# Weight conversion of the first quarter from attention tile 12 instead of 18, in a one-core attention and two-MoE kernel

## The chip, the cores and the metric

The kernel runs on one core of a Trainium2 chip. The metric is the device time of one execution in microseconds, given as the median of several runs. A profiled execution has its own time and, beside it, the span from its first to its last instruction.

## The reference

Clustered attention feeds a dense MoE block, which feeds a routed MoE block with eight experts.

```python
attn: B=2, H=8, S=768, D=64
  mask   = q_assign[:, :, :, None] == k_assign[:, :, None, :]   # argmax over 16 centroids
  scores = where(mask, q @ k.T / sqrt(D), -1e9)
  attn   = softmax(scores) @ v                                  # -> x of 1536 x 512
moe:   x = (relu(x @ w_in) ** 2) @ w_out                        # w_in 512 x 2048, float64
moe2:  do_compute = x @ w_skip > 0;  e = argmax(x @ w_gate)
       y = prob[e] * (relu(x @ w1[e]) @ w2[e]);  out = x + y
```

## The kernel before, in words

**Attention.** The 16 heads (two batches of eight) are handled two at a time, as 8 pairs of 12 tiles, 96 tiles of 128 queries by 768 keys. A loop over i (line 683) writes the order of every engine's work by hand: `ORDER` (line 24) lists the operations of one turn. In turn i, PE makes the scores of tile i + 3 (`S`, line 513), DVE takes their row maximum nm (`M`, line 520), ACT the exponential p (`E`, line 529). Of tile i itself PE transposes both halves into PSUM tiles pt (line 555; three PSUM tiles in rotation), ACT rounds them to ph (line 569), DVE takes the rest pl (line 578), and PE multiplies both with the values (line 588). Every 12 turns the operands of the next pair are prepared in between: PE transposes q and k (line 342), ACT copies them out (line 430), POOL splits them (lines 134 and 350), DVE finds the clusters (lines 380, 382, 399), POOL splits v (lines 134 and 413). Every third turn an output block is copied by ACT (lines 604, 605) and for the second head scaled by POOL (lines 607, 608). In attention PE, ACT, DVE and POOL keep the hand-written order; the order of SP's queue of transfers is set by a planner.

**Conversion of weights.** `weights` (line 183) is a generator that turns float64 weights of the first MoE block into a high and a low part, in four quarters of four units. A unit is 17 steps: for a w_in block and then for a w_out block, one step each for the transfer into a staging tile st (line 157, three staging tiles), one ACT operation (line 164), four DVE operations (lines 166, 169, 171, 174), the high part and the low part on POOL (lines 134 and 180); the 17th step closes the unit. The first quarter's 68 steps are spread over 96 turns: 17 steps in 24 turns (line 666, operation `D`, which comes after the values' first matmuls and before the second half's transposes).

```python
            if op == "D" and i >= CONV0:
                convert((i + 1) * CONV1 // 96 - i * CONV1 // 96)
```

The loop runs to i = 98. From line 693 on the last turns also split the attention's output for the first MoE block (line 230), and from i = 92 they do its first two steps (line 248 into sc).

**First MoE block.** A loop over 64 steps s (line 1107) makes, with PE, a hidden block (`gemm1`, lines 248 to 251), then two steps later its product with w_out (`gemm2`, line 1091). Step s of the first chunk needs unit s + 1 of the weights. After each step five more conversion steps are written (line 1116), until all four quarters are done. Here PE alone keeps its written order, and a planner orders ACT, DVE, POOL and SP, which may put an operation of this block between those of the attention's last turns. A staging transfer from step 3 on is held back by a one-element ACT copy (line 155).

**The rest.** Routing, and then eight experts, whose weights are loaded once the routing has named the first expert.

Of the kernel before, what the change touches and what calls it, by code (L numbers as in the profile page):

```python
# [28 lines left out]
SCALES = 1  # L29
SLAG = 2  # L30
ALB = 2
CONV0 = 18
CONV1 = 68
WARM = (9,1,1,2,2,2,4)
LOOK = 3
# [17 lines left out]
def clustered_attention_moe(  # L53
# [147 lines left out]
    def convert(n):  # L201
        for _ in range(n):
            if next(wgen, None) == "unit":
                wdone[0] += 1
# [57 lines left out]
    with ExitStack() as actx:  # L262
# [270 lines left out]
        def scales(n, c):  # L533

            su = su_t.pop((n, c)).rearrange("p t (h o) -> p t h o", o=1)
            nc.vector.tensor_scalar_add(su, su, 1e-9)
            nc.vector.reciprocal(out=su, in_=su)
            rr = sc_g[n, c] = alp.tile([128, G], F32, name="rr", bufs=2)
            nc.vector.tensor_copy(out=rr.rearrange("p (t h d) -> p t h d", t=GT, h=2),
                                  in_=su.to_broadcast([128, GT, 2, 64]))  # L540
# [93 lines left out]
        def micro(op, i):  # L634
# [26 lines left out]
            if op == "Z":  # L661
                m = i + LA - SLAG
                if 0 <= m < NQ and tiles[m][1] == 1 and m % GT == GT - 1:
                    scales(tiles[m][0], m // GT % 2)
            if op == "D" and i >= CONV0:
                convert((i + 1) * CONV1 // 96 - i * CONV1 // 96)
# [599 lines left out]
```

## Time and profile before

| what | us |
|---|---|
| median of 3 runs | 686.53 |
| lowest and highest run | 683.21, 688.05 |
| the profiled execution | 684.3 |
| its span | 682.5 |

The share of the granted TensorE clock is 0.989 over the span. Attention fills the span up to about 266 us, the first MoE block to about 530 us, the experts the rest. Busy time is that of an engine's own instructions; idle time before an instruction is put down to what released it. PE, DVE, ACT and POOL are the matmul, vector, scalar and GpSimd engines, and SP's queue issues most transfers.

### The profile page before, as it was taken

Reading aid. Unit: us, or ns where it says so; the run is one execution under the profiler, and the core shown is the slowest. Engines: PE = TensorE matmul, PEld = TensorE weight load, DVE = VectorE, ACT = ScalarE, POOL = GpSimd, SP = SyncE. Lnnn points to the kernel's source line nnn. Section 1 sums busy time; section 2 is a strip of 40 time slices with the busy share of each in tenths; the row PEclk is TensorE's granted clock in tenths of the full one; section 3 lists DMA queues with packets and bytes.
Section 4 is the critical chain, followed back from the end, with each engine's and each line's share of the span. In section 5 each row is a group of like instructions: output and inputs, shape, how many; then the busy total and the mean of one; then the engine's idle time right before and its main releaser. Section 6 shows DMA issues by size and latency. Waiting matters only on the chain. (4 is left out here: it accounts for less than half of the span.)

```text
span 682.5 us, 11258 instructions
## 1 busy us (share of the span) xinstructions
PE 648.4 (95%) x3769; PEld 566.0 (83%) x3769; DVE 477.4 (70%) x928; ACT 415.7 (61%) x846; POOL 253.7 (37%) x329
## 2 busy tenths in 40 slices
PE   7899899999999998999999999999999797999994
PEld 6788888989898887999998999999888575888883
DVE  4787899999999999654456455522244688899950
ACT  5799889989998984544433333322323375778830
POOL 4816264544736346643343443511010103113110
PEclk9899999999999999999999999999999989999998
DMA  5867764665746100123122312101222697999900
GB/s 130 190 150 154 185 142 122 150 157 127 164 123 139 41 1 9 63 66 104 63 78 62 108 63 62 40 0 47 93 93 94 216 315 252 345 356 362 367 13 23
DMA packets 72034, 89.90 MB, mean 132 GB/s; under 512 B 32384, under 2 KB 43584, under 8 KB 71968
## 3 DMA queue, kind: packets, MB, share of 16 engines
q1 hardware_dynamic: 68096, 84.12, 42.5%
q0 software_dynamic: 1440, 3.01, 1.3%
q10 hardware_dynamic: 2432, 1.97, 0.9%
q8 instruction: 32, 0.52, 0.3%
q14 instruction: 34, 0.28, 0.1%
HBM read 62.18 MB, written 9.44 MB: 105 GB/s over the span
## 5 line engine op out<-in xcount | busy, mean ns | idle before, releaser
L578 DVE TENSOR_TENSOR pl<-pt,ph 128x384 fp32r<-128x384 f32 x192 | 103.5, 551 | 19.2 <-ACT ph L569 18.0
L255 ACT ACTIVATE r<-hps 128x384 f32<-128x384 f32 x62 | 30.5, 492 | 120.7 <-PE hps L248 115.7
L555 PE MATMUL pt<-ident,p 128*128 128x128 f32 x576 | 95.9, 276 | 3.9 <-DVE pl L578 2.8
L513 PE MATMUL sc<-B,A 80*128 80x384 f32 (+1 forms) x384 | 91.8, 361 | 2.0 <-ACT p L529 1.8
L569 ACT CAST ph<-pt 128x384 fp32r<-128x384 f32 x192 | 89.7, 481 | 6.6 <-PE pt L555 5.9
L520 DVE TENSOR_REDUCE nm<-sc 128x1 f32<-128x768 f32 x96 | 91.0, 948 | 2.5 <-PE sc L513 2.5
L258 DVE TENSOR_TENSOR hl<-r,hh 128x384 fp32r<-128x384 f32 x62 | 36.7, 591 | 76.4 <-POOL hh L134 76.0
L529 ACT ACTIVATE p<-sc,nm 128x768 f32<-128x768 f32 x96 | 87.3, 910 | 4.4 <-DVE nm L520 4.3
L555 PEld LDWEIGHTS pt<-ident,p 128*128 128x128 f32 x576 | 70.4, 141 | 18.3 <-DVE pl L578 10.9
L134 POOL TENSOR_SCALAR hh<-r 128x384 fp32r<-128x384 f32 x62 | 35.4, 571 | 134.3 <-ACT r L256 114.9
L1091 PE MATMUL acc<-woh,hh 128*128 128x512 f32 x186 | 74.3, 400 | 0.0
L1091 PE MATMUL acc<-wol,hh 128*128 128x512 f32 x186 | 73.5, 395 | 0.0
L588 PE MATMUL av<-ph,vs 128*128 128x384 f32 x192 | 73.0, 380 | 0.1
L1091 PE MATMUL acc<-woh,hl 128*128 128x512 f32 x186 | 72.9, 392 | 0.0
L513 PEld LDWEIGHTS sc<-B,A 80*128 80x128 f32 (+1 forms) x384 | 63.2, 191 | 6.3 <-ACT p L529 6.2
L588 PE MATMUL av<-pl,vs 128*128 128x384 f32 x192 | 65.2, 339 | 0.6 <-DVE pl L578 0.6
L248 PE MATMUL hps<-A,wil 128*128 128x384 f32 x184 | 61.9, 336 | 2.0 <-POOL wil L180 2.0
L248 PE MATMUL hps<-A,wih 128*128 128x384 f32 x184 | 62.4, 339 | 0.0
L248 PE MATMUL hps<-B,wih 128*128 128x384 f32 x184 | 61.9, 337 | 0.0
L164 ACT ACTIVATE u<-st 128x512 f32<-128x512 f32 x32 | 21.7, 677 | 32.9 <-DMA st<-in_moe_w_in_dram 25.6
L1091 PEld LDWEIGHTS acc<-woh,hl 128*128 128x128 f32 x186 | 35.2, 189 | 7.8
L1091 PEld LDWEIGHTS acc<-woh,hh 128*128 128x128 f32 x186 | 35.2, 189 | 5.7 <-DVE xc L1099 0.2
(260 smaller groups left out, 1484.1 us busy)
## 6 DMA issues: line engine op xcount, KB each, us to landing
xc<-in_moe_w_dram SPq DMA_DIRECT2D x34, 512.0 KB, 5.5
st<-in_moe_w_dram SPq DMA_DIRECT2D x30, 512.0 KB, 5.8
st<-in_moe_w_in_dram SPq DMA_DIRECT2D x64, 128.0 KB, 2.9
st<-in_moe_w_out_dram SPq DMA_DIRECT2D x16, 512.0 KB, 3.9
A<-hi SPq DMA_DIRECT2D x30, 192.0 KB, 3.5
B<-hi SPq DMA_DIRECT2D x30, 192.0 KB, 4.0
qn<-in_q_dram SPq DMA_DIRECT2D x16, 192.0 KB, 3.5
vn<-in_v_dram SPq DMA_DIRECT2D x16, 192.0 KB, 2.6
```

The costliest lines, as they stand in the source:

```text
L134: nc.gpsimd.tensor_scalar(out=o, in0=i, scalar1=1.0, scalar2=0.0, op0=ALU.mult, op1=ALU.add)
L248: nc.tensor.matmul(out=hps, lhsT=wi[w][:, c, f * 128:(f + 1) * 128], rhs=xhl[ch][a][:, c], start=(n == 0), stop=(n == 3 * KD - 1))
L255: nc.scalar.activation(out=r, in_=hps, func=AF.Relu)
L258: nc.vector.tensor_tensor(out=hl, in0=r, in1=hh.bitcast(F32), op=ALU.subtract)
L513: nc.tensor.matmul(out=sc[:, c, 0:384], lhsT=A[h][0:kk, a, t * 128:(t + 1) * 128], rhs=Bk[h][0:kk, a, c * 384:(c + 1) * 384], start=(a == ...
L520: nc.vector.tensor_reduce(out=nm_t[i], in_=sc_t[i][:, :, 0:384], op=ALU.max, axis=AX.XY, negate=True)
L529: nc.scalar.activation(out=p, in_=sc[:, :, 0:384], func=AF.Exp, bias=nm, scale=1.0, accum_out=su_t[n, c][:, t, h:h + 1])
L555: nc.tensor.transpose(out=pt[:, c], in_=p_t[i][:, n, c * 128:(c + 1) * 128], identity=ident)
L569: nc.scalar.copy(out=block(i, n)[by_pool].bitcast(F32) if by_pool else block(i, n)[0], in_=pt_t[i, n])
L578: nc.vector.tensor_tensor(out=pl, in0=pt_t.pop((i, n)), in1=ph.bitcast(F32), op=ALU.subtract)
L588: nc.tensor.matmul(out=av, lhsT=vs[:, c, 2 * h:2 * h + 2].rearrange("p x d -> p (x d)"), rhs=r[:, c], start=(c == 0 and i == 0), stop=(c = ...
L1091: nc.tensor.matmul(out=acc, lhsT=h2[a][:, i * 128:(i + 1) * 128], rhs=wo[w][:, f], start=(f == 0 and n == 0), stop=(f == NF - 1 and n == 2))
```

## The change

The constant that says in which turn of the attention's loop the conversion begins goes from 18 to 12. The pace, 17 steps in 24 turns, stays.

```diff
-CONV0 = 18
+CONV0 = 12
 CONV1 = 68
```

## Rows read from the trace of the kernel before

**Rows 1.** The page, part 1: busy us (share of the span) xinstructions.

```profile
PE 648.4 (95%) x3769; PEld 566.0 (83%) x3769; DVE 477.4 (70%) x928; ACT 415.7 (61%) x846; POOL 253.7 (37%) x329
```

**Rows 2.** Waits, 241.9 to 275 us: us in total, times, longest.

```profile
PE hps L248 <- POOL wil L180: 2.0, 1, 2.0
```

**Rows 3.** Timeline, PE, 270.6 to 273.5 us: start, length, instruction, idle before.

```profile
270.69 0.33 PE L248 MATMUL hps<-A,wih 128*128 128x384 f32 x1
273.03 0.44 PE L248 MATMUL hps<-A,wil 128*128 128x384 f32 x1 [2.01 <-POOL wil L180]
```

**Rows 4.** Timeline, DVE then POOL, 256 to 273 us.

```profile
259.69 0.42 DVE L169 TENSOR_SCALAR l<-st 128x512 int32<-128x512 int32 x1
...
263.13 1.41 DVE L171 SCALAR_TENSOR_TENSOR l<-st,l 128x512 int32<-128x512 int32 x1
...
267.79 0.99 DVE L174 SCALAR_TENSOR_TENSOR u<-u,l 128x512 int32<-128x512 int32 x1
...
269.12 0.79 POOL L134 TENSOR_SCALAR wih<-u 128x512 fp32r<-128x512 f32 x1
...
271.26 1.71 POOL L180 TENSOR_TENSOR wil<-u,wih 128x512 fp32r<-128x512 f32 x1
```

**Rows 5.** Windows, stretches of six turns, then the tail and the MoE block.

```profile
core 0: us, PE busy (x) PEld busy (x) DVE busy (x) ACT busy (x) POOL busy (x), PEclk, DMA share, GB/s
...
61.50:77.00 15.50, 13.98 (x94) 12.95 (x93) 12.33 (x23) 13.40 (x32) 5.96 (x10) 1.00 0.69 156
77.00:93.70 16.70, 15.86 (x111) 13.60 (x109) 15.79 (x28) 14.71 (x35) 8.37 (x10) 1.00 0.71 175
93.70:107.60 13.90, 13.90 (x96) 12.89 (x95) 13.04 (x24) 13.42 (x32) 7.23 (x11) 1.00 0.53 123
107.60:123.30 15.70, 15.55 (x110) 13.41 (x109) 15.07 (x28) 14.49 (x35) 8.82 (x10) 1.00 0.60 141
123.30:137.00 13.70, 13.70 (x94) 12.70 (x93) 12.25 (x23) 13.23 (x32) 7.20 (x11) 1.00 0.62 145
...
241.90:255.00 13.10, 12.57 (x77) 11.17 (x78) 12.98 (x25) 11.40 (x27) 5.40 (x7) 1.00 0.01 2
255.00:266.40 11.40, 10.83 (x67) 9.47 (x65) 10.62 (x23) 8.14 (x18) 3.77 (x5) 1.00 0.01 1
...
275.00:330.00 55.00, 55.00 (x279) 50.03 (x278) 29.29 (x51) 24.00 (x53) 26.53 (x32) 1.00 0.25 77
```

**Rows 6.** Timeline, DVE: the four conversion operations of unit 2's w_in block.

```profile
138.37 0.42 DVE L166 TENSOR_SCALAR u<-u 128x512 f32<-128x512 f32 x1
...
140.49 0.94 DVE L169 TENSOR_SCALAR l<-st 128x512 int32<-128x512 int32 x1
...
143.92 1.37 DVE L171 SCALAR_TENSOR_TENSOR l<-st,l 128x512 int32<-128x512 int32 x1
...
149.36 0.68 DVE L174 SCALAR_TENSOR_TENSOR u<-u,l 128x512 int32<-128x512 int32 x1
```

**Rows 7.** Timeline, POOL: one split of v, one output scaling.

```profile
126.17 0.74 POOL L413 TENSOR_TENSOR vs<-vn,vs 128x256 fp32r<-128x256 f32 x1
...
143.74 1.00 POOL L607 TENSOR_TENSOR xc<-xc,al 128x384 f32<-128x384 f32 x1 [2.59 <-ACT xc L605]
```

**Rows 8.** Timeline, PE: where it stood idle between 137 and 153.7 us.

```profile
142.73 0.55 PE L555 MATMUL pt<-ident,p 128*128 128x128 f32 x3 [0.21 <-DVE pl L578]
...
145.81 0.55 PE L555 MATMUL pt<-ident,p 128*128 128x128 f32 x3 [0.47 <-DVE pl L578]
```

**Rows 9.** Timeline, SP's queue and PE, 41.6 to 47 us.

```profile
41.66 1.31 SPq L293 DMA_DIRECT2D qn<-in_q_dram  x2
...
45.96 1.85 SPq L157 DMA_DIRECT2D st<-in_moe_w_in_dram  x4
46.23 0.52 PE L342 MATMUL tp<-ident,qn 128*128 128x128 f32 x3 [0.48 <-DVE pl L578]
```

**Rows 10.** Timeline, ACT: the first conversion operation.

```profile
70.87 0.68 ACT L164 ACTIVATE u<-st 128x512 f32<-128x512 f32 x1
```

## The prediction, made before the changed kernel ran

> **What bounds the kernel now.** I read the page first, then the waits around the end of attention, then windows of six turns, then the timeline of single engines. On the page PE is busy for 95% of the span [rows 1], so time can only be won where PE stands still, and lost where another engine makes it stand still. In the first MoE block PE never stops: 55.00 busy us in 55.00 [rows 5]. Whatever the change moves there is hidden, as long as the weights are there in time.
>
> At one place they are not. At 270.69 PE begins the block's step 3, which needs unit 4 of the weights, and then waits 2.01 us for its low part [rows 2, 3]. That low part is conversion step 59. The attention's loop writes 58 steps; the last ones come late: the DVE operations at 259.69, 263.13 and 267.79, the high part at 269.12, the low part at 271.26 for 1.71 us [rows 4]. The wait is set by where these steps are written, not by a transfer.
>
> In attention the windows fall into two kinds. From turn 21 on, six turns with the operands' preparation at their heart (turns 9 to 2 of 12, "heavy") take 16.70 or 15.70 us, and the six others ("light") take 13.90 or 13.70. In the light ones PE is busy all the time, DVE for 12.25 to 13.04 us and ACT for 13.23 to 13.42: three engines near their limit. In the heavy stretch of 16.70 PE stands still for 16.70 - 15.86 = 0.84 us [rows 5], and in the same stretch one pair later PE's idle places are two waits for pl, just behind two conversion operations that took 0.94 and 1.37 us [rows 6, 8]. The heavy stretch of 15.70 has hardly any idle.
>
> **The change part by part.** Step k is written in the first turn i in which the count of (i + 1) x 68 / 96 reaches k + 12 before, and k + 8 after. So every step moves up by four steps, between five and seven turns, and the loop writes 62 steps instead of 58.
>
> *What moves where.* Before, the w_in block's four DVE steps lay in turns 21, 22, 23 and 25, the w_out block's in 32, 33, 35 and 36, and so on every 24 turns: seven of eight in heavy stretches. After, they lie in 15, 16, 18 and 19, and in 26, 28, 29 and 31: seven of eight in light ones. ACT's operation goes the other way, from turns 19 and 31 to 14 and 25.
>
> *Heavy stretches that held a w_in block* (the row at 77.00, two more of the pattern at 137.00 and 197.10). They lose three or four DVE operations and keep or gain one of 0.42. PE's 0.84 idle us should go, and the stretch come to the 15.70 of its neighbour: 1.0 less. But ACT gains 0.68 us [rows 10] on 14.71, which makes 15.39 in 15.70, so I take 0.8. Three times: -2.4. Bounds: 0 (ACT takes over) and -3.0.
>
> *The other heavy stretches* lose DVE work that PE did not wait for and gain 0.68 us of ACT on 14.49: 15.17 in 15.70. A light stretch now runs with ACT at the same share without a PE stop. I take 0, with bounds -0.3 and +0.5 in all.
>
> *Light stretches that get a w_in block* (turns 39 to 44, row 123.30; two of them, and turns 15 to 20, row 61.50). The four DVE steps cost 0.42 + 0.42 + 0.69 + 0.68 = 2.2 us undisturbed, with 0.69 for line 171 as the half of its 1.37, near line 174's 0.68; or 0.42 + 0.94 + 1.37 + 0.68 = 3.4 as in rows 6. DVE's room is 13.70 - 12.25 = 1.45 us. So DVE lacks 0.75 to 1.95 us. Some is lent by the neighbours, since three transposed tiles are in flight, and the stretch loses 0.68 us of ACT work, for which DVE waits there. I take 0.6 each, bounds 0 and 2.0; the stretch at 61.50 has 15.50 - 12.33 = 3.2 of room and takes 0.3. Sum: +1.5.
>
> *Light stretches that get the rest of a w_out block* (row 93.70, three of them). They get 0.42 + 0.69 + 0.68, lose one operation of line 166, 0.42, and have 13.90 - 13.04 = 0.86 of room: lacking 0.5, or 1.7 if disturbed. I take 0.3, bounds 0 and 1.7. Sum: +0.9.
>
> In these light stretches POOL splits v, in pieces of 0.74 us, and scales outputs in pieces of 1.00 [rows 7]. In rows 6 and 7 the operation of 1.37 us ran beside such a scaling, at 143.92 and 143.74. The Trainium skill (SBUF — State Buffer, Who interferes with whom) has a DVE operation with two SBUF inputs, or one in a two-port mode, wait for the whole of a POOL instruction that began before it. By that rule lines 166 and 169, moved beside the split of v, would lose up to 0.74 us each, and the light w_in stretch would lack about 2.2 us. It speaks against the change, and the mechanism of the slower rival below is the same, worked out from rows.
>
> *The last full stretch* (turns 87 to 92, row 241.90). DVE is busy 12.98 of 13.10 us there, with the split of the attention's output beside its own work. It now gets the four DVE steps of unit 4's w_in block: 2.2 less 0.12 of room, +2.1. Nothing hides it, since DVE is the bound there. Bounds: +0.5 (the low part of the unit before it, on POOL, leaves the stretch, so DVE may run less disturbed) and +3.3.
>
> *The tail* (row 255.00). Those steps leave it. PE stood idle there for 11.40 - 10.83 = 0.57 us: -0.5, bounds 0 and -0.6.
>
> *The wait for unit 4.* Steps 58 and 59 are now written in turns 93 and 94, so the low part is ready before attention's matmuls end: -2.0. PE's next need, step 2's squares, is freed at the same time, as POOL no longer has the 0.79 and 1.71 us of rows 4 ahead of them. What follows is bound by PE, and the experts' loads start after the routing, so the gain is kept. Bounds: -2.0 and 0.
>
> *SP's queue.* Nothing keeps SP's written order, but the staging transfers stay between the same two loads of q, k and v: the first is written in turn 12, after the load of turn 7 and before that of turn 19. The queue's first four staging issues took 1.85 us right behind that load, and the load's q was just late, with PE idle for 0.48 us [rows 9]. I take 0, bounds 0 and +1.85.
>
> Sum: -2.4 + 0 + 1.5 + 0.9 + 2.1 - 0.5 - 2.0 = -0.4 us. Against the profiled execution's 684.3 that is 683.9. That execution lies 2.2 below the median of 686.53, so for a median I say 686.1.
>
> **The rivals.**
>
> *All hidden.* The lookahead lends DVE all it lacks: light stretches 0, last stretch +0.5. Then -2.4 + 0.5 - 0.5 - 2.0 = -4.4: 682.1. For it speaks that PE ran at 100% with DVE at 13.04 of 13.90; against it, that ACT and DVE are both near full there.
>
> *DVE becomes the bound of the light stretches.* Each moved operation meets POOL and is prolonged as in rows 6. Then w_in stretches lose 2.0 twice and 0.2 once, w_out stretches 1.7 three times, the last stretch 3.3, and the tail gives nothing: 4.2 + 5.1 + 3.3 - 2.4 - 2.0 = +8.2: 694.7, slower. It decides from the point where a light stretch grows past about 15 us. Against it: POOL is busy for only about 7.2 us of a light stretch, and some of that was its conversion work, which moves away.
>
> *The change doesn't do what it says.* The planner already lifts block-one work into attention's last turns; if it then puts other POOL work ahead of the low part, the wait stays: -0.4 + 2.0 = +1.6: 688.1.
>
> *SP's order.* The first staging transfer goes ahead of the load that is just late: -0.4 + 1.85 = +1.5: 688.0.
>
> **How the numbers follow.** Forecast 0.58, all hidden 0.20, DVE bound 0.12, the other two 0.05 each. Since 1%, about what a measurement of this kernel can tell from no change, is 6.9 us, only the DVE rival at its full price passes it, and the hidden one only if the measured median also falls low (the three runs lie 4.8 us apart). So faster 0.06, within 1% 0.84, slower 0.10. The range reaches down below the hidden case and up to where the DVE rival is half paid: 681.0 to 692.0.
>
> **What would show it.** Right: no wait of PE on line 180 near 270 us; heavy stretches all near 15.7 to 15.9; light ones 14.0 to 14.5, with PE's idle there put down to pl or ph; the stretch from the 91st row maximum some 2 us longer. Wrong: light stretches still at 13.7 to 13.9 (all hidden), or past 15 with DVE at 100% (DVE bound); heavy ones still at 16.7, which would mean that line 169 and line 171 were not the cause of PE's idle; a wait of PE on line 342 near 46 us longer than 0.48.

## The result, and the profile after

The changed kernel takes 693.83 us (median of 6 runs, 691.94 to 696.01) against 685.43 for the kernel before (6 runs): 1.0124 times, with an interval of 1.0099 to 1.0148. It is 8.4 us slower, and the forecast of 686.1 with a range up to 692.0 missed it. The profiled execution of the changed kernel took 696.01 us, with a span of 694.2.

On the page PE's busy time hardly moves; the span grows around it (as [rows 1]).

```profile
PE 652.2 (94%) x3769; PEld 568.5 (82%) x3769; DVE 479.1 (69%) x928; ACT 417.6 (60%) x845; POOL 253.4 (37%) x329
```

The windows of the changed kernel, cut at the starts of every sixth row maximum (the same turns as in [rows 5]; the columns are the same):

```profile
core 0: us, PE busy (x) PEld busy (x) DVE busy (x) ACT busy (x) POOL busy (x), PEclk, DMA share, GB/s
...
63.44:79.80 16.36, 14.25 (x92) 12.41 (x91) 14.83 (x27) 13.11 (x31) 6.70 (x11) 1.00 0.60 145
79.80:97.29 17.49, 16.18 (x115) 14.18 (x113) 14.96 (x26) 15.96 (x38) 9.38 (x11) 1.00 0.74 177
97.29:111.19 13.90, 13.01 (x88) 11.69 (x87) 13.69 (x26) 12.45 (x29) 6.88 (x11) 1.00 0.66 171
111.19:127.56 16.37, 16.21 (x116) 14.41 (x115) 13.73 (x24) 15.11 (x36) 7.97 (x10) 1.00 0.60 133
127.56:141.95 14.39, 13.51 (x90) 11.80 (x89) 14.11 (x27) 13.01 (x31) 6.91 (x11) 1.00 0.61 152
141.95:159.76 17.81, 16.41 (x118) 14.60 (x116) 15.04 (x26) 15.97 (x38) 9.36 (x11) 1.00 0.61 135
...
251.15:265.40 14.25, 12.65 (x76) 10.96 (x76) 14.25 (x27) 11.30 (x26) 5.65 (x8) 1.00 0.12 37
265.40:277.50 12.10, 11.22 (x59) 10.16 (x60) 8.86 (x20) 6.36 (x14) 3.76 (x5) 0.86 0.00 1
```

The reader is to see three things. The light stretches went about as forecast: those with the rest of a w_out block stayed at 13.90, with DVE at 13.69 (97.29), and those with a w_in block grew to 14.39, with DVE at 14.11 (127.56). The heavy ones that held a w_in block did the opposite of the forecast: instead of falling from 16.70 to 15.9 they grew to 17.49 and 17.81, though DVE does less in them (15.04 where it did 15.79). And the last full stretch has DVE busy for the whole 14.25.

From turn 21 on a stretch repeats to a few hundredths in the runs whose conversion steps lie in the same turns there: turns 21 to 26 took 16.69 in the kernel before and in two runs below (e8, e9), and 17.49 and 17.48 in the changed kernel and another (e7). Earlier ones do not: turns 9 to 14 took 17.20 in the kernel before, and 17.08 to 17.91 in four runs below that have the same steps as it up to turn 16 (e8 to e11). With that in mind the loss can be laid out by stretches, as the difference of the starts of two row maxima six tiles apart in the timeline (line 520):

| turns | 9-14 | 15-20 | 21-26 | 27-32 | 33-38 | 39-44 | 45-50 | 51-56 | 57-62 | 63-68 | 69-74 | 75-80 | 81-86 |
|---|---|---|---|---|---|---|---|---|---|---|---|---|---|
| before | 17.20 | 15.50 | 16.69 | 13.88 | 15.68 | 13.75 | 16.71 | 13.86 | 15.70 | 13.77 | 16.72 | 13.39 | 14.72 |
| after | 17.81 | 16.36 | 17.49 | 13.90 | 16.38 | 14.39 | 17.80 | 13.91 | 16.37 | 14.38 | 17.79 | 13.90 | 15.04 |

The differences add up to +7.95. From turn 87 to the last values' block (the 187th matmul of line 588 with ph) it is 23.94 against 21.05, +2.89. From the first matmul of the MoE block's step 2 to the first of its step 5 (line 248, hps from A and wih, the 1st and the 13th) it is 14.33 against 14.88, -0.55. What lies between and what follows is equal to 0.1. Before turn 9 the two profiled executions differ by 1.3 us; that part varies between kernels with the same start as well (first row maximum at 15.6 to 17.9).

PE stands still at two places in the stretch of turns 45 to 50. First PE's rows, then what DVE, POOL and ACT did just before, all of the changed kernel's timeline:

```profile
148.37 0.55 PE L555 MATMUL pt<-ident,p 128*128 128x128 f32 x3 [0.70 <-DVE pl L578]
...
158.42 0.52 PE L555 MATMUL pt<-ident,p 128*128 128x128 f32 x3 [0.70 <-DVE oh L382]
```

```profile
145.58 0.84 DVE L536 TENSOR_SCALAR su<-su 128x6 f32<-128x6 f32 x1
146.46 0.19 DVE L537 RECIPROCAL su<-su 128x6 f32<-128x6 f32 x1
146.75 1.10 DVE L539 COPY rr<-su 128x384 f32<-128x384 f32 x1
...
155.79 0.56 DVE L578 TENSOR_TENSOR pl<-pt,ph 128x384 fp32r<-128x384 f32 x1 [1.41 <-ACT ph L569]
...
157.71 0.56 DVE L382 TENSOR_TENSOR oh<-lg,mx 128x384 bf16<-128x384 f32 x1
...
145.38 1.01 POOL L350 TENSOR_TENSOR lo<-qf,hi 128x384 fp32r<-128x384 f32 x1
146.35 1.28 POOL L180 TENSOR_TENSOR wil<-u,wih 128x512 fp32r<-128x512 f32 x1
...
154.73 0.66 ACT L164 ACTIVATE u<-st 128x512 f32<-128x512 f32 x1
155.29 0.47 ACT L569 CAST ph<-pt 128x384 fp32r<-128x384 f32 x1
```

The first wait: the w_in block's low part, now in turn 46, runs on POOL from 146.35 to 147.63, and DVE's copy of the scales, begun at 146.75, takes 1.10 us. The operation on line 536 takes 0.84, beside POOL's split of q (line 350). In the kernel before the copy took 0.36 and line 536 took 0.16; there it was the conversion operation of line 169 that ran beside this split and took 0.94 [rows 6]:

```profile
141.36 0.16 DVE L536 TENSOR_SCALAR su<-su 128x6 f32<-128x6 f32 x1
...
141.85 0.36 DVE L539 COPY rr<-su 128x384 f32<-128x384 f32 x1
```

The Trainium skill (SBUF — State Buffer, Who interferes with whom) says that a DVE operation in a two-port mode, which a copy with fitting operands can enter, and a GpSimd one exclude each other, and that the later waits for the whole of the earlier. By that rule the copy would end at about 147.63 + 0.36 = 147.99, an estimate; the trace has 147.85, near it. In which mode this copy runs, the trace doesn't tell. The reciprocal just before it ran its usual 0.19 beside the same POOL operation. The prediction looked for such meetings at the moved operations, not at the scales. The second wait: ACT's conversion operation, now in turn 49, stands ahead of ph; DVE waits 1.41 us for ph, and everything behind it, the clusters' operations too, is late.

In the light stretch of turns 39 to 44 the four moved operations themselves ran undisturbed or nearly so:

```profile
128.89 0.49 DVE L166 TENSOR_SCALAR u<-u 128x512 f32<-128x512 f32 x1
...
131.10 0.41 DVE L169 TENSOR_SCALAR l<-st 128x512 int32<-128x512 int32 x1
...
135.77 0.68 DVE L171 SCALAR_TENSOR_TENSOR l<-st,l 128x512 int32<-128x512 int32 x1
...
138.17 0.68 DVE L174 SCALAR_TENSOR_TENSOR u<-u,l 128x512 int32<-128x512 int32 x1
```

### The profile page after: what moved, and what is told of

Read it like the earlier page. It is cut to its first block, busy times and chain, and to the rows that moved or that the text cites. A ratio compares the mean times of both kernels' runs of the same rounds, so it can differ in the third digit from the quotient of the medians.

```text
span 694.2 us, 11265 instructions
## 1 busy us (share of the span) xinstructions
PE 652.2 (94%) x3769; PEld 568.5 (82%) x3769; DVE 479.1 (69%) x928; ACT 417.6 (60%) x845; POOL 253.4 (37%) x329
## 3 DMA queue, kind: packets, MB, share of 16 engines
q1 hardware_dynamic: 68096, 84.12, 41.6%
## 5 line engine op out<-in xcount | busy, mean ns | idle before, releaser
L134 POOL TENSOR_SCALAR hh<-r 128x384 fp32r<-128x384 f32 x62 | 37.2, 600 | 142.1 <-ACT r L256 122.9
```

What stands on the lines that cost most here:

```text
L134: nc.gpsimd.tensor_scalar(out=o, in0=i, scalar1=1.0, scalar2=0.0, op0=ALU.mult, op1=ALU.add)
```

## The experiments

The loop's line was replaced by a table that says in which turns a block of eight steps takes its next one. With the turns of either kernel in the table the instructions and their order are that kernel's on every engine, and all lines keep their numbers.

```diff
-            if op == "D" and i >= CONV0:
-                convert((i + 1) * CONV1 // 96 - i * CONV1 // 96)
+            for b in PLAN.get(i, ()) if op == "D" else ():
+                next(blocks[0, b // 2, b % 2] if blocks else wgen)
```

The turns of unit 1 (24 more for each further unit) are, for transfer, ACT, DVE's four, high part, low part:

```
before  w_in  18 19 21 22 23 25 26 28   w_out 29 31 32 33 35 36 38 39
after   w_in  12 14 15 16 18 19 21 22   w_out 23 25 26 28 29 31 32 33
```

The stretches of one unit in all runs that bear on them, then the way from turn 87 to the last values' block, and from the first matmul of the MoE block's step 2 to the first of its step 5 (us):

| | before | after | e1 | e2 | e3 | e5 | e6 | e9 | e10 | e12 |
|---|---|---|---|---|---|---|---|---|---|---|
| 39-44 light | 13.75 | 14.39 | 13.69 | 14.40 | 15.30 | 14.40 | 14.40 | 13.69 | 13.87 | 14.40 |
| 45-50 heavy | 16.71 | 17.80 | 17.12 | 17.50 | 17.10 | 17.05 | 16.75 | 15.71 | 15.66 | 15.97 |
| 51-56 light | 13.86 | 13.91 | 13.88 | 13.91 | 13.76 | 13.90 | 13.90 | 13.69 | 13.88 | 15.42 |
| 57-62 heavy | 15.70 | 16.37 | 16.07 | 15.99 | 16.41 | 16.40 | 15.99 | 15.72 | 15.70 | 16.00 |
| 87 to end | 21.05 | 23.94 | 21.58 | 24.09 | 24.63 | 22.50 | 24.07 | 21.04 | 21.03 | 22.50 |
| MoE steps | 14.88 | 14.33 | 14.71 | 14.25 | 14.34 | 14.33 | 14.13 | 17.77 | 17.02 | 14.11 |

**ACT alone (e1_act_moved).**

```diff
-w_in  18 19 21 22 23 25 26 28   w_out 29 31 32 33 35 36 38 39
+w_in  12 14 21 22 23 25 26 28   w_out 23 25 32 33 35 36 38 39
```

> The kernel before, with ACT's conversion operation (and its transfer) alone written in the turns of the changed kernel (14, 25, 38, 49, 62, 73, 86); DVE's and POOL's steps stay. Theory (each of ACT's operations costs its whole 0.67 us in a heavy stretch): 3 to 4.7 us slower than before, and heavy stretches without other change longer by 0.7 each. Rival (the loss comes from DVE's operations in the light stretches): within 0.5 us of before.

688.66 us, 1.0047 times the kernel before (1.0017 to 1.0077). Every heavy stretch grew by 0.37 to 0.47; the light ones grew by no more than 0.05. In turns 45 to 50 PE's second wait, 0.69 us behind the clusters' oh, is already there. ACT's move alone costs 2.9 us; each operation costs a little more than half of its 0.67, not all.

**ACT back (e2_act_back).** Blocks 3 to 7 of the changed kernel have ACT's operation in turns 31, 43, 55, 67, 79, and their transfers two turns before.

> The changed kernel, with ACT's conversion operation of the third to seventh block written in light stretches (turns 31, 43, 55, 67, 79 in place of 38, 49, 62, 73, 86). Theory: 5 x 0.67 = 3.3 us faster than the changed kernel, so some 690.5, heavy stretches shorter by 0.7 each. Rival (DVE in light stretches): no faster than the changed kernel, or slower, since the light stretches get more to do.

691.72 us, 1.0084 (1.0053 to 1.0115): about 2.1 less than the changed kernel, not 3.3. The five heavy stretches that lose ACT's operation lose 0.29 to 0.57 each, and the light ones, where ACT's work now lies, stay at 14.40 and 13.91.

**POOL's steps of units 1 to 3 back (e3_pool_back).**

```diff
-w_in  12 14 15 16 18 19 21 22   w_out 23 25 26 28 29 31 32 33
+w_in  12 14 15 16 18 19 26 28   w_out 23 25 26 28 29 31 38 39
```

> The changed kernel, with POOL's high and low part of the first three units written in the turns of the kernel before (26 and 28, 38 and 39, and so on, in place of 21 and 22, 32 and 33). Theory (the low part in turns 22, 46 and 70 prolongs the scales on DVE, and PE waits 0.7 us each time): about 2 us faster than the changed kernel, no wait of PE on pl near the 50th row maximum. Rival (DVE or ACT alone): within 0.5 us of the changed kernel.

694.29 us, 1.0121 (1.0086 to 1.0155): nothing won. The stretches say why. Turns 45 to 50 are 0.70 shorter, as the theory had it, but 39 to 44 are 0.91 longer: there the w_out block's low part on POOL now stands beside the next block's first DVE operation, which takes 1.37 us, and the second, later by that, meets a split of v and takes 0.83, against 0.49 and 0.41 for the same two in the changed kernel. For units 1 to 3 this run has ACT and POOL in the turns of e1. So 694.29 - 688.66 = 5.6 us is the price of DVE's move, together with that of unit 4's steps, which differ on POOL as well; the two aren't separated.

**The low part alone (e5_low_part_later).**

```diff
-w_in  12 14 15 16 18 19 21 22
+w_in  12 14 15 16 18 19 21 28
```

> The changed kernel, with POOL's low part of the w_in blocks of units 1 to 3 alone written six turns later (28, 52, 76 in place of 22, 46, 70). Theory (that low part runs beside the scales on DVE and PE waits 0.7 us for it, three times): stretches of turns 21-26, 45-50 and 69-74 0.7 us shorter each, the light ones as in the changed kernel, 2 us faster than it. Rival (POOL's work costs wherever it stands, as the run with all of POOL's steps back suggests): what the heavy stretches win the light ones lose, within 0.5 us of the changed kernel.

692.05 us, 1.0091 (1.0069 to 1.0114): 1.8 less than the changed kernel. Turns 45 to 50 take 0.75 less, and all other stretches of the table stay. The gain is the copy's: it takes 0.36 again, 0.74 less, while line 536 is as long as in the changed kernel.

```profile
144.51 0.84 DVE L536 TENSOR_SCALAR su<-su 128x6 f32<-128x6 f32 x1
...
145.69 0.36 DVE L539 COPY rr<-su 128x384 f32<-128x384 f32 x1
```

**Both repairs (e6_act_and_low_part).**

> The changed kernel, with both repairs: ACT's operation of the third to seventh block in light stretches, and the low part of the w_in blocks six turns later. Theory (the two costs add up): 2 + 2 = 4 us faster than the changed kernel, some 689.7; what is left over the kernel before, some 4 us, is DVE's operations in light stretches and in the last full one. Rival (ACT, DVE and POOL cover each other): less than 3 us faster than the changed kernel.

689.57 us, 1.0043 (1.0022 to 1.0064): 4.3 less than the changed kernel. The costs add up: 45 to 50 fall by 0.30 + 0.75 to 16.75. But that is still a whole microsecond over the 15.71 of the next run, and no conversion operation on DVE but one of line 166 is in it.

**No conversion in turns 42 to 65 (e9_unit2_out).**

> The kernel before, with no conversion step in turns 42 to 65 (unit 2 takes the turns of unit 3; units 3 and 4 are left to the MoE block, which will wait for them). Theory (a w_in block's DVE operations cost the heavy stretch of turns 45-50 about 1 us, a w_out block's nothing): turns 45-50 at 15.7 us, 57-62 at 15.4 to 15.7, light ones as before. Rival (the heavy stretches of 16.7 and 15.7 differ by the preparation itself): 45-50 still above 16.3.

One execution, 688.47. Without conversion a unit's stretches take 13.69, 15.71, 13.69 and 15.72. So both heavy stretches are alike, the w_in block cost the kernel before 1.00 us there, and the changed kernel's 17.80 is 2.1 us over what the stretch takes without conversion.

**The last of the 2.1 us (e12_maxmin_later).** As e6, with line 166 of the w_out blocks in turns 27, 51, 75.

> The kernel of the run e6_act_and_low_part, with the first DVE operation of the w_out blocks (line 166) one turn later (27, 51, 75 in place of 26, 50, 74). Theory (there it stands behind the clusters' two operations and beside the output scaling on POOL): turns 45-50 go from 16.75 to about 15.8, turns 51-56 grow by no more than 0.3. Rival (something else lengthens that stretch): 45-50 above 16.4.

One execution, 693.53. The stretch falls to 15.97, so the operation of line 166 in turn 50 was 0.78 of the whole microsecond that e6 left. In e6 it ran beside an output scaling on POOL (that this meeting, and not its place alone, makes the 0.78 is not shown):

```profile
155.44 0.95 DVE L166 TENSOR_SCALAR u<-u 128x512 f32<-128x512 f32 x1
...
155.09 1.01 POOL L607 TENSOR_TENSOR xc<-xc,al 128x384 f32<-128x384 f32 x1 [2.90 <-DVE oh L382]
```

But the next stretch grew by 1.52, past the 0.3 that was expected: in turn 51 the operation met the low part of the w_in block, which this kernel has in turn 52, and took 1.35 us; the next one, of line 169, took 0.82 instead of 0.42. Moving one operation by one turn moved its price along.

**DVE in better places (e10_same_places).** The kernel before, with the w_in blocks in the places of the w_out blocks.

```diff
-w_in  18 19 21 22 23 25 26 28
+w_in  17 19 20 21 23 24 26 27
```

> The kernel before, with the w_in blocks written in the same places of the 12 turns as the w_out blocks (DVE in 20, 21, 23, 24 in place of 21, 22, 23, 25, POOL in 26 and 27 in place of 26 and 28). Theory (which turns the DVE operations stand in decides): the heavy stretches with a w_in block go from 16.7 to about 15.7, three times, 2 to 3 us faster than the kernel before, some 683. Rival (a w_in block costs there in any case, as its transfers are four): within 0.7 us of before.

683.63 us, 0.9971 (0.9944 to 0.9999): faster than both kernels, if by little. From turn 21 to 74 all heavy stretches are at 15.66 to 15.73 now, three times 1.0 us won. The same four operations, one turn earlier but for the third, cost nothing (POOL's low part went one turn back too, from 28 to 27, a light stretch in both kernels). DVE isn't less busy by it: with line 536 these operations take 0.90 + 0.41 + 0.67 + 0.68 + 0.98 = 3.64 us here and took 0.42 + 0.94 + 0.16 + 1.37 + 0.68 = 3.57 before. What changed is which of them is long. Line 171 began 0.18 us after an output operation of POOL in the kernel before and took 1.37 [rows 6, 7]; here it begins 0.10 before that, takes 0.68, and POOL's takes 1.45:

```profile
143.37 0.68 DVE L171 SCALAR_TENSOR_TENSOR l<-st,l 128x512 int32<-128x512 int32 x1
...
143.47 1.45 POOL L607 TENSOR_TENSOR xc<-xc,al 128x384 f32<-128x384 f32 x1 [2.54 <-DVE pl L578]
```

The MoE block's first steps take 2.1 us back in the profiled execution, 17.02 against 14.88; the runs below are about them.

**Everything 12 turns earlier (e4_twelve_earlier).**

> The kernel before with every step written 12 turns earlier (the first transfer 15), so that each engine's steps keep their places within the 12 turns of a pair, and 66 steps lie in attention. Theory (the places cost, not the earlier begin): as the kernel before in all stretches, without the 2 us wait on line 180: 683 to 685. Rival (each step more in attention costs there): 687 to 690.

687.07 us, 1.0024 (1.0002 to 1.0045): 1.3 slower than before, between the two. The stretches with a w_in block and those with a w_out block change places (15.73 for 16.69 in turns 21 to 26, 16.70 for 15.68 in 33 to 38), so the places decide there. Turns 81 to 86, which had no w_in block before, take 1.04 us more, turn 87 to the end takes 1.2 less. Turns 9 to 14 take 1.24 more, but in e8, which moves nothing there, they take 0.71 more too. The wait on line 180 is gone, but the MoE steps are only 0.2 shorter, and the block behind them, up to the last hidden steps, takes 2.1 us more, with PE waiting for hh (1.20 us at 279.28), and later for DVE's line 1099.

**Unit 4 as before (e7_unit4_as_before).** The changed kernel with the first seven steps of unit 4's w_in block in turns 90, 91, 93, 94, 95, 97, 98, and the rest of the unit after the loop.

> The changed kernel, with the conversion of unit 4 written in the turns of the kernel before (90 to 98; 58 steps in attention). Theory (unit 4's four DVE operations in the last full stretch cost about 3 us there and bring back only 0.5 at the first MoE steps): about 2.5 us faster than the changed kernel, the 2 us wait on line 180 back. Rival (the last stretch is as long anyway): 0 to 1.5 us slower than the changed kernel.

691.85 us, 1.0099 (1.0076 to 1.0122): 2.0 less than the changed kernel. From turn 87 on it takes 20.27 instead of 23.94 (or 22.50 in e5, at full clock), and PE waits 1.95 us for the low part again. Unit 4's earlier place costs more than it brings.

**The wait on line 180 by itself (e8_unit4_quicker).** The kernel before, unit 4's last six steps in turns 92 to 97.

```diff
-unit 4, w_in  90 91 93 94 95 97 98
+unit 4, w_in  90 91 92 93 94 95 96 97
```

> The kernel before, with the last six steps of unit 4 in turns 92 to 97, one in each, the low part with them. Theory (POOL has too much to do just after attention, and when the wait on line 180 goes another takes most of its place): 0 to 1 us faster than the kernel before. Rival (the wait is worth its whole length): 2 us faster than before, 683.5.

684.97 us, 0.9995 (0.9970 to 1.0019): no change that can be measured, and the first MoE steps take 15.47 against 14.88. The wait of [rows 3] is gone, and two others stand in its place, in PE's timeline of this run:

```profile
279.20 0.50 PE L1091 MATMUL acc<-woh,hh 128*128 128x512 f32 x1 [1.33 <-POOL hh L134]
...
280.88 0.50 PE L1091 MATMUL acc<-woh,hl 128*128 128x512 f32 x1 [0.95 <-DVE hl L258]
```

In e10 they are there too, with 1.45 and 0.95 us, and its windows show POOL busy without a gap before and up to them:

```profile
264.00:269.00 5.00, 5.00 (x27) 4.42 (x26) 4.96 (x6) 2.10 (x5) 5.00 (x7) 1.00 0.00 0
269.00:274.00 5.00, 5.00 (x28) 4.61 (x27) 4.62 (x5) 1.97 (x5) 5.00 (x5) 1.00 0.26 84
274.00:279.00 5.00, 2.59 (x10) 1.75 (x9) 2.19 (x3) 0.55 (x2) 4.42 (x6) 0.90 0.28 100
279.00:284.00 5.00, 5.00 (x21) 4.36 (x21) 4.72 (x10) 1.41 (x3) 0.90 (x2) 0.75 0.01 2
```

**POOL relieved (e11_pool_first).**

```diff
-        do(early_h), convert_to(PLAN_UNITS)
+        do(early_h), convert_to(PLAN_UNITS), convert(1)
...
-        if ps + 1 < NPASS:
+        if ps + 1 < NPASS and s > 2:
             convert(5)
```

> The kernel of the run e10_same_places, with step 59 written at once after attention, and the five conversion steps after each of the MoE block's steps 0, 1 and 2 left out (they follow at step 3). Theory (POOL is the bound of the first MoE steps: conversion work stands ahead of the squares' high part): PE's waits for hh and hl at those steps go, 1.5 to 3 us faster than e10, some 681. Rival (the split of the second chunk and the output scalings hold POOL anyway): within 0.7 us of e10.

683.61 us, 0.9972 (0.9953 to 0.9992): as e10, and as the rival had it. PE's waits for hh and hl are gone, and the one on line 180 is back, at 3.06 us. On POOL the split of the second chunk (vs) and two output operations now stand ahead of the low part:

```profile
273.50 0.69 PE L248 MATMUL hps<-A,wil 128*128 128x384 f32 x1 [3.06 <-POOL wil L180]
...
267.27 2.50 POOL L134 TENSOR_SCALAR vs<-xc 128x384 fp32r<-128x384 f32 x3
269.74 1.42 POOL L607 TENSOR_TENSOR xc<-xc,al 128x384 f32<-128x384 f32 x1
271.24 0.99 POOL L608 TENSOR_TENSOR xc<-xc,rr 128x384 f32<-128x384 f32 x1
272.19 1.26 POOL L180 TENSOR_TENSOR wil<-u,wih 128x512 fp32r<-128x512 f32 x1
```

So in these three orders (the kernel before, e8 and e10, e11) another of POOL's results is late, but one always is. It fits that POOL's work in these few microseconds is the bound; a run that takes the split or the output operations off POOL there was not made.

## Why the prediction was wrong

The size of the loss is that of the rival "DVE becomes the bound of the light stretches" (694.7), but that is chance: its mechanism is not what happened. From turn 21 on the light stretches stayed at 13.9 to 14.4 and never passed 15, and the moved operations took 0.49, 0.41, 0.68 and 0.68 us in turns 39 to 44, close to the undisturbed 2.2 of the forecast. Lines 166 and 169 did stand beside the splits of v, but met only the last 0.21 and 0.06 us of the POOL operations that had begun before them. Taken by its own steps:

- *Heavy stretches that held a w_in block*, forecast -2.4, were +0.80, +1.09 and +1.07, so +2.96. This is the step that failed, by 5.4 us. It took PE's idle time as gone with the operations behind which it stood, asked of ACT's newcomer only whether its busy time still fits, and did not ask about POOL's newcomers at all: the high and the low part moved from turns 26 and 28 to 21 and 22. The busy times fit, and all the same a stretch without a conversion step takes 15.71 (e9) and this one 17.80: 0.30 for ACT's operation ahead of ph (e2), 0.75 for the low part beside the scales (e5), 0.78 for line 166, which ran beside an output scaling (e12) and had been counted as 0.42, and 0.26 unexplained. That the departing DVE operations were worth 1.0 was right (e9). With ACT's move made first, taking them away and bringing line 166 into turn 50 left the stretch as it was (e3 against e1: 17.10 and 17.12).
- *The other heavy stretches*, forecast 0, were +0.70, +0.67 and +0.32, so +1.69. The reason "a light stretch runs with ACT at the same share without a PE stop" fell with e1: an ACT operation costs a heavy stretch some 0.4 with ACT busy for 15.07 of 16.07 us. Taking it out again gave back 0.37 of the 0.70 and 0.38 of the 0.67 (e2); the 0.3 that stays in each is unexplained.
- *Turns 9 to 14*, which had no term, were +0.61. That says nothing: e8 has +0.71 there with the steps of the kernel before.
- *Light stretches with a w_in block*, forecast +1.5: +0.86, +0.64, +0.61, so +2.11. Right in kind, with DVE busy for 14.11 of 14.39 us. The first was the one mis-sized (0.3 forecast): PE's wait of 1.51 us on line 342 in it stayed, at 1.69, and line 166 took 0.98. That DVE's room lay behind this wait fits, but no run was made on it.
- *Light stretches with the rest of a w_out block*, forecast +0.9, 0.3 each: +0.02, +0.05, +0.51, so +0.58. The sum is about right; two of the three hid the operations altogether.
- *The last full stretch and the tail*, forecast +2.1 - 0.5 = +1.6: +2.89 in the profiled execution, +1.45 in e5 and e12, which leave unit 4's DVE and POOL steps as the changed kernel has them. Right but for the clock (below). In e5 all of the 1.45 lies in the last full stretch (14.27 against 12.80 between the 91st and the last row maximum); the tail's -0.5 did not come.
- *The wait for unit 4*, forecast -2.0, brought 0.55. The low part was early, as forecast, but the sentence that the squares are freed at the same time was wrong. In the changed kernel PE waits for the next results instead, 0.29 us for line 255's and 0.84 us for hl, and in e8 removing the wait won nothing at all.
- *SP's queue*: 0 forecast. PE's wait on line 342 near 46 us went from 0.48 to 0.68, which the prediction had named as a sign of being wrong. It isn't one: with the steps of the kernel before the same wait is 0.40 to 1.19 (e8 to e11). In the kernel before the profile puts this wait down to pl, in the changed one to the transfer of q; so the reading of [rows 9], that q was just late, isn't what its row says. Nothing is shown against the 0.

```profile
291.25 0.50 PE L1091 MATMUL acc<-woh,hl 128*128 128x512 f32 x1 [0.84 <-DVE hl L258]
```

Without turns 9 to 14 the terms measured sum to 2.96 + 1.69 + 2.11 + 0.58 + 1.45 - 0.55 = 8.2 at full clock in the tail, and to 9.7 with the 2.89 of the profiled execution. The medians differ by 8.4, with an interval of 6.8 to 10.1. One reading of the prediction is off without consequence: [rows 8] lie two pairs, not one, behind the row at 77.00.

## What to carry to other kernels

Where three engines work in lockstep, the busy share of a stretch says little on what one more operation costs there: the same four DVE operations cost 1.0 us or nothing depending on one turn (e10). Before operations are moved in such a schedule, look up in the timeline, for each new place, what waits behind it on its own engine and what the neighbour engine runs beside it. Do so for every step that moves, the short ones on ACT and POOL too. And a single late result just behind a phase boundary is worth its wait only if the next results are not late too.

## What the runs showed of the hardware

TensorE's granted clock fell after a wait in some executions and not in others. In the tail of the changed kernel PE was busy 2.96 us of 4.50, with waits of 1.43 and 0.60, and the clock of that window and the next was 0.72 and 0.90; e5, with the same work and waits of 1.42 and 0.60 there, kept 1.00. Of the six profiled executions with unit 4's DVE and POOL steps as the changed kernel has them, the clock fell there in four (the changed kernel, e2, e3, e6) and not in two (e5, e12). First the windows of the changed kernel, then those of e5:

```profile
260.10:264.60 4.50, 4.01 (x27) 3.59 (x25) 4.50 (x10) 3.79 (x10) 2.81 (x4) 1.00 0.36 117
264.60:269.10 4.50, 2.96 (x12) 2.62 (x13) 3.79 (x7) 1.59 (x4) 1.48 (x2) 0.72 0.00 0
269.10:273.50 4.40, 4.40 (x29) 4.29 (x28) 3.65 (x10) 2.33 (x6) 0.00 (x0) 0.90 0.00 0
```

```profile
262.00:266.70 4.70, 3.09 (x20) 2.77 (x21) 4.56 (x9) 1.84 (x4) 1.55 (x2) 1.00 0.00 0
266.70:271.30 4.60, 4.60 (x32) 4.17 (x30) 4.19 (x12) 3.79 (x9) 0.97 (x2) 1.00 0.00 0
```

A mean of 0.72 is a mix of the two levels, 1.2 and 2.4 GHz. The fall cost 23.94 - 22.50 = 1.4 us from turn 87 to the end.

The same happened in the first MoE steps. In e7 the clock fell after PE's wait of 1.95 us on line 180; in the kernel before, with the same steps and a wait of 2.01 us, it didn't, and these steps took 14.88 us instead of 16.42. First the window of e7, then that of the kernel before:

```profile
279.90:284.30 4.40, 4.37 (x15) 4.08 (x16) 2.85 (x4) 2.76 (x6) 4.23 (x4) 0.61 0.00 0
```

```profile
273.00:277.40 4.40, 4.37 (x22) 3.98 (x23) 2.84 (x4) 2.92 (x6) 4.23 (x4) 1.00 0.00 0
```

In e10 the fall followed the waits for hh and hl (0.90 and 0.75 in the windows above). With the same two waits e8 kept its clock, so about 17.02 - 15.47 = 1.5 of the 2.1 us that e10 lost in these steps is the clock. So a wait of PE can cost more than its own length.
